# Output stores issued two products later in a fused attention and MLP kernel

## The chip, the cores and the metric

The kernel runs on one core of a Trainium2 chip. The time is device time in microseconds from one launch to its end; lower is better. The engines named below are TensorE (matrix products; PE in the profile, PEld for its weight loads), VectorE (DVE), ScalarE (ACT), GpSimd (POOL) and SyncE (SP). SyncE does no arithmetic here: it issues nearly all transfers between the memories, one after another, in the order in which the program wrote them. An engine runs its own list in order and meets the others only at semaphores.

## The reference

Eight batches of attention with 12 heads, 448 tokens and 64 elements a head, with q and k normalised by their root mean square, followed by a two-layer MLP on the joined heads:

```python
q_n, k_n = rmsnorm(q, g_q), rmsnorm(k, g_k)
attn = softmax(q_n @ k_n.T / sqrt(64)) @ v        # 8 x 12 x 448 x 64
x = attn.transpose(0, 2, 1, 3).reshape(3584, 768)
h = x @ w_in                                      # 768 -> 2048
g = h - tanh(h)
out = g @ w_out                                   # 2048 -> 768
```

All inputs and the output are float32 (in the kernel's launch, float64 weights are handed over as pairs of 32-bit words and rounded on the chip).

## The kernel before

The program writes all engines' lists out in one pass, without a scheduler. It goes over 48 attention steps, one for a batch and a pair of heads, and between the pieces of a step it lets a generator, `mlp`, put so many matrix products of an earlier batch into TensorE's list. So the MLP of batch b stands between the attention of batch b+1, and the MLP of the last batch stands alone at the end.

**The MLP.** For the first batch the projection is computed plainly (`project_first`): six chunks of 128 output columns, each of sixteen matrix products (L939), turned and stored one after another. During it the second half of the weights is still being rounded: SyncE loads raw words (L276), ScalarE, VectorE and GpSimd work on them in turn (L71, L78 to L82, L90), and the finished factors are copied out to memory (L359).

For the other batches both layers are computed by a scheme of seven products instead of eight: the rows of `ORDER`, 1, 5, 6, 2, 3, 7, 4, run through `products` (matmuls on L774). A hidden set is one run through the seven, with six matrix products in each; there are four sets in a batch. A projection has three runs with eight in each. A matrix product shows as two instructions in the profile. Each product needs a weight tile that is loaded from memory into one of six slots in a ring. At the start of product n the program writes the load of the tile of product n+4 into SyncE's list (`ring_load`, L397 for the first layer and L399 for the second). Since there are six slots, that load waits until TensorE has finished product n-2.

**The stores.** A projection run makes two chunks of 128 output columns. The first is complete after product 3, the second after product 4. What remains to be done for a chunk is put into `late["todo"]`, and runs after the matmuls of the following product have been written. It is `store`: VectorE turns the chunk in blocks of 32 by 32 (L869) into a tile `th`, of which there are two in rotation, and SyncE issues four transfers to the output (L872), of which the first waits for the turn. In SyncE's list they stand where the program is at that moment, so everything written later, whether a weight tile, v (L115, L125) or q and k (L462), is issued after them. The same two `th` tiles are used for tanh in the hidden layer (L810), and ScalarE waits there for a store that still reads its tile.

**What else hangs on SyncE.** q and k of a later step are loaded by eight transfers (L462), the first of which waits until VectorE has scaled the step whose buffer they take (L495). Each transfer also waits for the one eight places before it, since eight semaphores go round.

Of the kernel before, what the change touches and what calls it, by code (L numbers as in the profile page):

```python
# [144 lines left out]
def bounded_path(tc, ctx, q, k, v, moe_w_in, moe_w_out, out, g_col, ident, ones, half_ones, neg_half, early):  # L145
# [17 lines left out]
    nc = tc.nc  # L163
    B, H, S, D = q.shape
    DFF, DM = moe_w_out.shape
    P = 128
    CP = S // NCH
    NP = H // 2
    CD, CF = DM // P, DFF // P
# [11 lines left out]
    BL = 32  # L181
# [4 lines left out]
    def pool(name, **kw):  # L186
        return ctx.enter_context(tc.tile_pool(name=name, **kw))
# [17 lines left out]
    def bank_of(name):  # L205

        turns[name] += 1
        return banks[name][turns[name] % len(banks[name])]

    def mm_bank():  # L210
        return bank_of("mm")
# [29 lines left out]
    def built(j, p):  # L241

        if j == 2:
            return ring[:, p * 2 * HALF : (p + 1) * 2 * HALF].rearrange("p (f n) -> p f n", f=2)
        return w_half[j == 1][p]

    def w_out_row(f, i):
        return w_half[i][f // 2][:, f % 2]
# [54 lines left out]
    def weight(to):  # L303

        while done[1] < min(to, PIECES):
            n = done[1]
            round_weight_a(nc, raws[n], weight_dst(n))
            if n:
                round_weight_b(nc, raws[n - 1], weight_dst(n - 1))
            done[1] = n + 1  # L310
            finish_weights(n)
            load_weights(n + (3 if n < EARLY - 3 else 4))
            if kept[1] < kept[0] and n >= 4 * kept[0] + 2:
                keep_weights()
        if done[1] == PIECES > done[2]:
            round_weight_b(nc, raws[PIECES - 1], weight_dst(PIECES - 1))
            finish_weights(PIECES)
# [15 lines left out]
    def combine(count):  # L333
        for j, p, dst, x, y, op in combos[:count]:
            nc.vector.tensor_tensor(out=dst, in0=x, in1=y, op=op)
            if p == 7:
                kept[0] = j + 1
        del combos[:count]
# [7 lines left out]
    def combine_w_out(f):  # L346

        a11, a21 = (w_out_row(f, i) for i in range(2))
        a12, a22 = (w_out_row(f + HF, i) for i in range(2))
        t = [ring_slot() for _ in range(2)]  # L350
        s3, s1, s2, s4 = (t[i // 2][:, i % 2 * HALF : (i % 2 + 1) * HALF] for i in range(4))
        nc.vector.tensor_tensor(out=s1, in0=a21, in1=a22, op=ALU.add)
        nc.vector.tensor_tensor(out=s3, in0=a11, in1=a21, op=ALU.subtract)
        nc.vector.tensor_tensor(out=s2, in0=s1, in1=a11, op=ALU.subtract)
        nc.vector.tensor_tensor(out=s4, in0=a12, in1=s2, op=ALU.subtract)
        late["keep"].append(lambda: [keep_factors(3 + 2 * i, 2, f, t[i]) for i in range(2)])
# [7 lines left out]
    def keep_w_out(n):  # L364

        if not CF <= n < PIECES:
            return
        f, i, src = weight_piece(n)
        if f >= HF or i == 0:
            blk = i + 1 if f >= HF else 0  # L370
            for r in range(2):
                keep_factors(blk, 1, f % HF + r, src[:, r])
# [3 lines left out]
    def ring_slot():  # L376
        n = slots[0] % SLOTS
        slots[0] += 1
        return ring[:, n * SLOT : (n + 1) * SLOT]
# [10 lines left out]
    def ring_load(to):  # L390

        for n in range(len(ring_tiles), min(to, len(ring_steps))):
            b, layer, j, p = ring_steps[n]
            t = ring_tiles[ring_steps[n]] = ring_slot()
            if layer == 0:
                assert kept[1] > j
                nc.sync.dma_start(out=t[:, : 2 * HALF], in_=w_in_dram[j, p])  # L397
            else:
                nc.sync.dma_start(out=t, in_=w_out_dram[:, BLOCKS[p], j].rearrange("p f d -> p (f d)"))  # L399
# [339 lines left out]
    late = {}  # L739
# [7 lines left out]
    def part(name):  # L747
        return tp.tile([P, 2, HS], F32, name=name)
# [4 lines left out]
    def products(b, layer, count, width, depth, moving, done_with):  # L753

        took = 4 * HS / ENGINE_NS
        banks = {}  # L760

        def product(j, p, bank, first):
            if b == 0:
                weight(due[7 * j + ORDER.index(p)])
                combine(1)
                while any(c[:2] == (j, p) for c in combos):
                    combine(1)
                w = built(j, p).rearrange("p f (n d) -> p (f n) d", d=P)
            else:
                ring_load(ring_steps.index((b, layer, j, p)) + 5)  # L770
                w = ring_tiles[b, layer, j, p].rearrange("p (n d) -> p n d", d=P)
            for f in range(width):
                for c in range(depth):
                    nc.tensor.matmul(  # L774
                        bank[:, f * HS : (f + 1) * HS], lhsT=w[:, c * width + f, :], rhs=moving[p](c),
                        start=(first and f == 0 and c == 0), stop=(f == width - 1 and c == depth - 1),
                        skip_group_check=not first,
                    )
                    if f < width - 1 or c < depth - 1:
                        yield took  # L780
            now = late["todo"]
            late["todo"] = []
            for fn in now:
                fn()

        for j in range(count):
            use = done_with(j)
            for p in ORDER:
                first = p not in (2, 3, 7)
                bank = banks[p] = mm_bank() if first else banks[{2: 1, 3: 5, 7: 6}[p]]  # L790
                yield from product(j, p, bank, first)
                use(p, bank)
                yield took
# [69 lines left out]
    def store(b, n, y):  # L863

        o = part("th").rearrange("p f s -> p (f s)")
        nc.vector.transpose(out=o, in_=y if b >= FIRST else y.rearrange("r (c p) -> r p c", c=NCH))  # L869
        for i in range(P // BL):  # L870
            d = n * P + i * BL
            nc.sync.dma_start(  # L872
                out=out[b * S : (b + 1) * S, d : d + BL].rearrange("(j t) d -> t j d", t=BL),
                in_=o[i * BL : (i + 1) * BL].rearrange("t (j d) -> t j d", d=BL),
            )

    def project(b):
        g, t = late["g"], late["t"]
# [33 lines left out]
    def project_first(b):  # L912

        g = late["g"]
        for fn in late["todo"]:
            fn()
        late["todo"] = []
        took = 4 * S / ENGINE_NS
        for m in range(CD * CF):
            k, f = m // CF, m % CF  # L920
            n = (k + HC) % CD
            if f == 0:
                bank = mm_bank()
            if k < HC:
                weight(CF + HF + HF * (m + 1) // (HC * CF))
            elif m < HC * CF + 2:
                keep_w_out(PIECES - 2 + m - HC * CF)
            elif (m - HC * CF) % 4 == 0 and m - HC * CF <= 4 * HF:
                for fn in late["keep"]:
                    fn()  # L930
                late["keep"] = []
                combine_w_out((m - HC * CF) // 4 - 1)
            elif m == CD * CF - 12:
                ring_load(2)
                for fn in late["keep"]:
                    fn()
            elif m == CD * CF - 10:
                ring_load(4)
            nc.tensor.matmul(  # L939
                bank[:, :S], lhsT=w_out_row(f, n // HC)[:, n % HC * P : (n % HC + 1) * P], rhs=g[:, f, :],  # L940
                start=(f == 0), stop=(f == CF - 1),
            )
            if f == CF - 1:
                y = part("s2").rearrange("p f s -> p (f s)")
                nc.scalar.copy(out=y, in_=bank[:, :S])
                store(b, n, y)
            yield took
        wp_stack.close()
        late["tg"] = pool("tg", bufs=1)
        late["blocks"] = pool("blocks", bufs=1)  # L950

    def mlp():
        late["todo"], late["keep"] = [], []
        for b in range(B):
            yield from hidden(b)
            yield from project(b) if b else project_first(b)
        for fn in late["todo"]:
            fn()

    stream = mlp()  # L960
    spent = [0.0, 0.0]

# [383 lines left out]
def kernel(  # L1346
# [77 lines left out]
    with tc.If(bounded) as cmp:  # L1424
        with ExitStack() as arm, tc.manual_schedule():
            bounded_path(tc, arm, q, k, v, moe_w_in, moe_w_out, out, g_col, ident, ones, half_ones, neg_half, early)
# [34 lines left out]
```

## Time and profile before

| quantity | value |
|---|---|
| three runs | 1387.53, 1391.36, 1393.45 us |
| median | 1391.36 us |
| profiled execution | 1391.79 us |
| its span, first to last instruction | 1390.0 us |
| TensorE busy | 1352.7 us |
| VectorE busy | 892.2 us |
| mean granted TensorE clock | 0.992 |
| output stores, L872 | 192 transfers of 56 KB, median 1.9 us to landing |
| w_in tiles, L397 | 196 transfers of 384 KB, median 3.6 us to landing |
| w_out tiles, L399 | 147 transfers of 512 KB, median 4.4 us to landing |
| share of the transfer engines' time in use, one queue | 65.8% |

The span is 1.8 us shorter than the time of the same execution, which also has what lies around the instructions. In a row of the profile, "line engine operation out<-in" names a group of instructions; in a row of waits the numbers are the us in total, the times and the longest in us. A timeline row has the start, the duration, and in brackets the idle time before it with what ended it. The engine SPq is SyncE's queue: its busy time there is that of issuing a transfer, not of the transfer.

### The profile page before, as it was taken

How to read it: one execution, taken by the hardware profiler on the slowest of the kernel's cores; microseconds unless marked ns; L12 is line 12 of the kernel's file. 1: busy time of each engine (PE TensorE's matmuls, PEld its weight loads, DVE VectorE, ACT ScalarE, POOL GpSimd, SP SyncE). 2: the span in 40 equal slices, each digit the busy share in tenths (PEclk: the TensorE clock that was granted, in tenths of full speed). 3: DMA queues.
4: the chain of work that ended last, by engine and by line, in shares of the span. 5: the costliest groups of instructions: out<-in, count | busy, mean ns of one | idle time of the engine just before them, and what ended most of it. 6: DMA issues, size and time to landing. Idle time of an engine off the chain costs nothing. (4 is left out here: it accounts for less than half of the span.)

```text
span 1390.0 us, 29929 instructions
## 1 busy us (share of the span) xinstructions
PE 1352.7 (97%) x11840; PEld 1128.9 (81%) x11840; DVE 892.2 (64%) x1378; ACT 552.3 (40%) x1314; POOL 554.8 (40%) x345
## 2 busy tenths in 40 slices
PE   7989899999999999999999999999999999999997
PEld 3458654478998898898889889988988988899997
DVE  4999888856864677567766568546775677533311
ACT  7855554244433443334433444334433344311100
POOL 4746565225632356224552346323562245302300
PEclk9999999999999999999999999999999999999999
DMA  7879788775667566666657756675666666456663
GB/s 174 193 211 245 250 232 214 211 194 153 172 175 191 156 177 180 170 144 201 187 134 178 199 149 174 182 183 155 179 177 172 148 206 177 108 181 185 192 192 90
DMA packets 367656, 249.90 MB, mean 180 GB/s; under 512 B 281748, under 2 KB 309780, under 8 KB 367508
## 3 DMA queue, kind: packets, MB, share of 16 engines
q1 hardware_dynamic: 367504, 247.90, 65.8%
q8 instruction: 96, 1.57, 0.5%
q14 instruction: 52, 0.43, 0.1%
q10 hardware_dynamic: 4, 0.00, 0.0%
HBM read 214.40 MB, written 33.42 MB: 178 GB/s over the span
## 5 line engine op out<-in xcount | busy, mean ns | idle before, releaser
L774 PE MATMUL mm<-xT,w_f 128*128 128x224 f32 x1392 | 275.6, 354 | 0.0
L774 PEld LDWEIGHTS mm<-xT,w_f 128*128 128x128 f32 x1392 | 262.2, 190 | 10.2 <-issue 10.2
L774 PEld LDWEIGHTS mm<-gT,w_f 128*128 128x128 f32 x1344 | 252.8, 190 | 12.8 <-issue 8.4
L774 PE MATMUL mm<-gT,w_f 128*128 128x224 f32 x1344 | 263.0, 354 | 0.0
L811 POOL TENSOR_TENSOR gT<-s,th 128x448 f32<-128x448 f32 x96 | 120.1, 1260 | 332.1 <-ACT th L810 331.8
L531 PE MATMUL sc<-qT,kT 64*32 64x448 f32 (+1 forms) x3072 | 217.3, 503 | 10.3 <-ACT p_last L537 9.3
L488 POOL TENSOR_TENSOR rr_mine<-rr_mine,neg_half 128x28 f32<-128x28 f32 x33 | 158.2, 4794 | 147.9 <-DVE rr_mine L486 97.1
L774 PE MATMUL mm<-tt,w_f 128*128 128x224 f32 x1044 | 208.9, 353 | 3.8 <-DMA w_f<-w_in 3.8
L774 PEld LDWEIGHTS mm<-tt,w_f 128*128 128x128 f32 x1044 | 196.7, 190 | 9.8 <-issue 6.3
L774 PE MATMUL mm<-tg,w_f 128*128 128x224 f32 x1008 | 197.5, 352 | 0.0
L774 PEld LDWEIGHTS mm<-tg,w_f 128*128 128x128 f32 x1008 | 190.7, 190 | 0.0
L531 PEld LDWEIGHTS sc<-qT,kT 64*32 64x32 f32 x3072 | 71.1, 107 | 78.8 <-issue 56.5
L712 DVE TENSOR_TENSOR xT<-xT,sc 128x448 f32<-128x448 f32 x35 | 21.7, 621 | 138.9 <-PE sc L531 94.7
L597 PE MATMUL sc<-p,v_nat 64*32 64x448 f32 x1120 | 110.5, 536 | 0.0
L734 POOL TENSOR_TENSOR tt<-xT,tt 128x224 f32<-128x224 f32 x23 | 31.2, 1357 | 168.9 <-DVE xT L716 147.1
L537 ACT ACTIVATE p<-sc 128x448 f32<-128x448 f32 x132 | 71.9, 545 | 51.5 <-PE sc L531 39.0
L687 ACT COPY sum_g<-sum 32x14 f32<-32x14 f32 x280 | 56.3, 201 | 56.2 <-DVE sum L679 44.9
L939 PE MATMUL mm<-gT,w_out 128*128 128x448 f32 x192 | 76.0, 551 | 0.3 <-POOL w_out L90 0.3
L810 ACT ACTIVATE th<-s 128x448 f32<-128x448 f32 x96 | 54.5, 573 | 49.4 <-DVE s L840 26.6
L939 PEld LDWEIGHTS mm<-gT,w_out 128*128 128x128 f32 x192 | 36.3, 193 | 38.3 <-issue 35.8
L597 PEld LDWEIGHTS sc<-p,v_nat 64*32 64x32 f32 x1120 | 40.6, 107 | 31.0 <-issue 31.0
L537 ACT ACTIVATE p_last<-sc 128x224 f32<-128x224 f32 x66 | 20.0, 355 | 113.9 <-PE sc L531 113.9
(151 smaller groups left out, 1858.7 us busy)
## 6 DMA issues: line engine op xcount, KB each, us to landing
w_f<-w_in SPq DMA_DIRECT2D x196, 384.0 KB, 3.6
w_f<-w_out SPq DMA_DIRECT2D x147, 512.0 KB, 4.4
w_raw<-in_moe_w_out_dram SPq DMA_DIRECT2D x16, 768.0 KB, 5.1
out_dram<-th SPq DMA_DIRECT2D x192, 56.0 KB, 1.9
w_in<-w_out SPq DMA_DIRECT2D x21, 384.0 KB, 5.9
qk_nat<-in_q_dram SPq DMA_DIRECT2D x132, 56.0 KB, 3.1
qk_nat<-in_k_dram SPq DMA_DIRECT2D x132, 56.0 KB, 2.5
v_nat<-in_v_dram SPq DMA_DIRECT2D x72, 96.0 KB, 3.7
```

The costliest lines, as they stand in the source:

```text
L488: nc.gpsimd.tensor_tensor(out=mine, in0=mine, in1=neg_half[:, :1].to_broadcast([P, 2 * NJ]), op=ALU.pow)
L531: nc.tensor.matmul(tiles[h][i * BL : (i + 1) * BL, :n], lhsT=kT[r, c * P + at : c * P + at + BL], rhs=qT[r, first : first + n], start=True ...
L537: nc.scalar.activation(p[:, h, c if c < 2 else 0, :], tiles[h][:, :n], AF.Exp, scale=1.0 if rr is None else rr[:, 0, 2 * c + h : 2 * c + h ...
L597: nc.tensor.matmul(av[g][i * BL : (i + 1) * BL, :S], lhsT=v_nat[keys, h, c, m * BL : (m + 1) * BL], rhs=p[keys, h], start=first, stop=True ...
L687: nc.scalar.copy(out=acc[h * BL : (h + 1) * BL, g], in_=part[g * BL : (g + 1) * BL, h * NJ : (h + 1) * NJ])
L712: nc.vector.tensor_tensor(out=x, in0=x, in1=av[1][:, :S], op=ALU.add)
L734: eng.tensor_tensor(out=t2, in0=x22, in1=t1, op=ALU.subtract)
L774: nc.tensor.matmul(bank[:, f * HS : (f + 1) * HS], lhsT=w[:, c * width + f, :], rhs=moving[p](c), start=(first and f == 0 and c == 0), sto ...
L810: nc.scalar.activation(th, h, AF.Tanh, bias=0.0, scale=1.0)
L811: eng.tensor_tensor(out=g[:, rows, cols], in0=h, in1=th, op=ALU.subtract)
L939: nc.tensor.matmul(bank[:, :S], lhsT=w_out_row(f, n // HC)[:, n % HC * P : (n % HC + 1) * P], rhs=g[:, f, :], start=(f == 0), stop=(f == C ...
```

## The change

The turn on VectorE stays where it is. The four transfers of a store are no longer written at once: they go into a list, `late["out"]`, with a count of two. At the start of each product of batches 2 to 8, just after the ring load of that product, every count goes down by one, and a store whose count is at zero is written. So a store stands behind the ring loads of the next two products. In the projection of the first batch the list is emptied in the middle of the next chunk, ahead of its ninth matrix product. What is left at the end of the MLP is written there.

```diff
             else:
                 ring_load(ring_steps.index((b, layer, j, p)) + 5)
+                step_out()
                 w = ring_tiles[b, layer, j, p].rearrange("p (n d) -> p n d", d=P)
...
         o = part("th").rearrange("p f s -> p (f s)")
         nc.vector.transpose(out=o, in_=y if b >= FIRST else y.rearrange("r (c p) -> r p c", c=NCH))
-        for i in range(P // BL):
-            d = n * P + i * BL
-            nc.sync.dma_start(
-                out=out[b * S : (b + 1) * S, d : d + BL].rearrange("(j t) d -> t j d", t=BL),
-                in_=o[i * BL : (i + 1) * BL].rearrange("t (j d) -> t j d", d=BL),
-            )
+
+        def issue():
+            for i in range(P // BL):
+                d = n * P + i * BL
+                nc.sync.dma_start(
+                    out=out[b * S : (b + 1) * S, d : d + BL].rearrange("(j t) d -> t j d", t=BL),
+                    in_=o[i * BL : (i + 1) * BL].rearrange("t (j d) -> t j d", d=BL),
+                )
+
+        late["out"].append([2, issue])
+
+    def step_out(by=1):
+        for entry in late["out"]:
+            entry[0] -= by
+        while late["out"] and late["out"][0][0] <= 0:
+            late["out"].pop(0)[1]()
...
             if f == 0:
                 bank = mm_bank()
+            if f == CF // 2:
+                step_out(2)
...
     def mlp():
-        late["todo"], late["keep"] = [], []
+        late["todo"], late["keep"], late["out"] = [], [], []
         for b in range(B):
             yield from hidden(b)
             yield from project(b) if b else project_first(b)
         for fn in late["todo"]:
             fn()
+        step_out(2)
```

On every engine but SyncE the order of the instructions is the same as before.

## The prediction

> **What bounds the kernel now.** I read the busy shares first.
>
> ```profile
> PE 1352.7 (97%) x11840; PEld 1128.9 (81%) x11840; DVE 892.2 (64%) x1378; ACT 552.3 (40%) x1314; POOL 554.8 (40%) x345
> ```
>
> TensorE sets the time, so the change is worth what it takes from, or adds to, TensorE's idle time and slow time after 203 us, where the first store is issued (the changed instructions start there). Next the windows, from 290 us (the second batch) to the last matmul, and the five us after the pause discussed below (columns: length, busy time of PE, PEld, DVE, ACT, POOL, granted clock, DMA share, GB/s):
>
> ```profile
> 290.00:1382.00 1092.00, 1087.92 (x9151) 969.31 (x9142) 655.35 (x1036) 388.64 (x1008) 402.88 (x245) 1.00 0.63 172
> ...
> 237.30:242.10 4.80, 4.80 (x20) 2.07 (x21) 4.59 (x8) 1.45 (x3) 4.01 (x4) 0.64 0.83 193
> ```
>
> In 1092 us TensorE idles 4.1 us: little is left there. TensorE's own waits (us in total, times, longest), and SyncE's queue's:
>
> ```profile
> PE sc L531 <- ACT p_last L537: 9.3, 3, 5.4
> ...
> PE mm L774 <- DMA w_f<-w_in: 3.8, 5, 2.0
> ```
>
> ```profile
> SPq L872 <- DVE th L869: 252.6, 45, 12.2
> ...
> SPq L462 <- DVE qk_n L495: 63.7, 16, 8.6
> ```
>
> SyncE stands 252.6 us before stores whose turn is not done, but TensorE loses only 3.8 us to late w_in tiles. The gain is bounded by TensorE's column, not SyncE's. By window, the five waits are 0.3, 2.0, 0.3, 0.8 and 0.3 us, one in each of five 180 us batches from 300 us on. All lie at the same place, the seventh product of a batch's first w_in set. The timeline of the last of them:
>
> ```profile
> 1103.72 1.09 DVE L495 TENSOR_TENSOR qk_n<-qk_nat,rr_mine 128x896 f32<-128x896 f32 x1
> 1104.73 0.64 DVE L869 STREAM_TRANSPOSE th<-s 128x448 f32<-128x448 f32 x1
> ...
> 1097.09 0.54 SPq L397 DMA_DIRECT2D w_f<-w_in  x1
> 1105.40 1.95 SPq L872 DMA_DIRECT2D out_dram<-th  x4
> 1107.45 0.44 SPq L397 DMA_DIRECT2D w_f<-w_in  x1
> 1107.98 1.95 SPq L462 DMA_DIRECT2D qk_nat<-in_q_dram  x4
> 1109.97 2.19 SPq L462 DMA_DIRECT2D qk_nat<-in_k_dram  x4
> 1112.27 6.42 SPq L397 DMA_DIRECT2D w_f<-w_in  x7
> ...
> 1115.83 2.51 PE L774 MATMUL mm<-tt,w_f 128*128 128x224 f32 x12 [0.32 <-DMA w_f<-w_in]
> ```
>
> SyncE issues a w_in tile at 1097.5, then stands to 1105.4 before the batch's last store (its turn is queued on VectorE behind the attention's work), then issues store, tile, eight q/k loads and at 1112.3 the tile that TensorE waits for at 1115.5.
>
> The other wait after 203 us is in the first batch:
>
> ```profile
> 223.97 2.04 POOL L90 TENSOR_TENSOR w_out<-w_out,w_raw 128x768 int32<-128x768 int32 x1 [2.27 <-ACT w_out L71]
> ...
> 221.72 0.37 SPq L276 DMA_DIRECT2D w_raw<-in_moe_w_out_dram  x1
> 222.19 2.14 SPq L872 DMA_DIRECT2D out_dram<-th  x4
> 224.43 1.84 SPq L115 DMA_DIRECT2D v_nat<-in_v_dram  x2
> 226.32 2.06 SPq L125 DMA_DIRECT2D v_nat<-in_v_dram  x2
> ...
> 229.64 0.46 SPq L276 DMA_DIRECT2D w_raw<-in_moe_w_out_dram  x1
> ...
> 234.81 0.89 ACT L71 ACTIVATE w_out<-w_raw 128x768 f32<-128x768 f32 x1 [6.47 <-DMA w_raw<-in_moe_w_out_dram]
> ...
> 237.30 1.23 PE L531 MATMUL sc<-qT,kT 64*32 64x448 f32 x14 [2.14 <-ACT p_last L537]
> ```
>
> A store and four v loads stand ahead of a raw weight load. ScalarE waits 6.47 us for that load, with the exponentials that free the score banks queued behind it, and TensorE waits 2.14 us. In the window from that point on, the granted clock is 0.64.
>
> **What the Trainium skill says.** "DMA: Bandwidth & Descriptors", section "Anatomy of one DMA", says that a semaphore wait happens on the issuing sequencer before dispatch. That is what the 8 us hole between 1097.6 and 1105.4 shows. "TensorE: Matmul & The Clock Gate", Part 1, says the clock is halved after an idle window of about 3.4 us, and full again after as long a busy one. The trace agrees on the size (0.64 over 4.8 us is 1.7 us lost, half of 3.4 us), but here 2.1 us of recorded idle was enough; I use the trace.
>
> **The change, part by part.** The store's four DMAs, their waits and their sizes stay; so do all orders on the other engines. Only SyncE's order changes.
>
> *Batch ends (batches 2 to 6, where attention still runs beside the next batch).* New order: three w_in tiles, the fourth, v, the fifth, the store of product 3's chunk, the sixth, q/k, the seventh, the last store. The earlier of the two stores is now ready when reached (its turn ended at 1091.64). The sixth tile needs only product 4 of the old batch (finished near 1096.3, as VectorE's L905 reads it then), the seventh product 1 of the new one (1105.7). The q/k loads still wait for VectorE's L495, which ends at 1104.8: SyncE's stand doesn't go, it goes over to them. Eight issues take 1.95 + 2.19 plus gaps, 4.2 us, so the seventh tile goes out near 1109.1 instead of 1112.3: 3.2 us earlier, where at most 2.0 us of idle is to be covered. In the worst batch one q issue is 1.7 us slow (3.68 against 1.95); the same 3.2 us remain, and 1.0 is spare. The five waits go: 3.8 us of idle, plus for each the overlap of matmul records, 354 ns long at a spacing of 189 (148.52 us for 784 in the chain): 5 x 0.16 = 0.8. **Sum 4.6 us.**
>
> What is late next: the last store's four issues (2.0 us) now stand ahead of the next set's first tile. It goes out near 1111.6 instead of 1112.8, so nothing moves later. The cover for its 3.6 us landing is product 4, which ends about 1118.2.
>
> *Between batch ends.* Stores in the middle of a projection also go behind two tiles. Where q/k loads come between, a following tile goes out up to 2.0 us (four issues) later than it would without the store; tiles go out about five products ahead (8 x 2 x 0.189 = 3.0 us each, 15 us), land after 4.4 us, and no wait stands there now. Cost 0. Without cover it would be 2 us each.
>
> *First batch.* The second store moves from ahead of the v loads to behind the q/k loads. The raw load then has four DMAs of v and two of w_out ahead: six issues at 0.5 to 0.6 us from 222.1, so 225.5; its buffer is free when POOL's L90 ends at 226.01. So 226.0 instead of 229.64: 3.6 us earlier. With the same 5.2 us to landing ScalarE gets it at 231.2, runs L71, L72, L945 and the exponentials (1.99 us from 234.81 to 236.80, then 0.79), limited by the score matmuls ending near 231.5, and is done near 234.0; TensorE needs it at 234.7. The pause goes, with 0.7 us to spare: 2.14 us plus the overlap of records there (536 ns long at 54 spacing), 0.5, so 2.6, plus 1.7 of half clock. **Sum 4.3 us.** The first store moves behind two raw loads that wait on POOL anyway (holes from 207.9 to 209.9 and 211.4 to 215.2), and lands well before its buffer is turned into again at 237.8. Later ones move among weight copies that no matmul near them reads: 0.
>
> *The end.* The last tiles are issued by 1365.1, so the late stores meet an empty queue; the last turn (1382.64) still precedes four issues of 2.12 us. 0.
>
> *Unknown: the stores' new company.* Each store writes 229 KB in 128-byte pieces right among weight loads; before, it often went out alone. From no effect (DMA share 0.63) to one tile late by the difference of longest and median landing of w_f, 8.1 - 4.1 = 4.0 us at each of five ends; a spare of 1.0 to 2.9 leaves 1 to 3 us in one or two ends, 0 to 4 us in all. I take 0.
>
> Total 8.9 us. Against the profiled execution's own 1391.79 this is 1382.9. That execution lies 0.4 us above the median of the runs shown, 1391.36; the forecast is **1383.0 us**. A measurement can tell about 0.5% (7 us) of this kernel from no change; 1384.4 is the line.
>
> **Rivals.**
>
> *Half the gain.* The first-batch pause depends on a landing under full DMA load (0.83) with 0.7 us to spare; a landing of 6 us brings it back, and any pause can halve the clock. Then only the 4.6 us go: 1387. For it: the fastest run, 1387.53, is 4.3 us under the profiled one, as if the pause weren't in every execution. Against: 3.6 us of lead. The same figure follows if the pause goes and the batch ends keep their waits.
>
> *The transfers are hidden anyway.* SyncE's wait goes to the q/k loads and the ring still comes late: 1390 to 1392. For it: the 8.6 us waits on L495 stay. Against: the 3.2 us worked out above, all of them issue time and a turn that no longer come first.
>
> *The change doesn't delay what it says.* If the countdown released stores in the same slot, nothing would move: 1391. Against: on SyncE's queue one or two tile loads, and the q/k group, change places with them.
>
> *A new wait, slower than before.* The last store's buffer (th, two of them) is next written by ScalarE's tanh, at 1114.05 now. The store is issued by about 1111.6 and lands after 1.9 us, at 1113.5: 0.5 us to spare. If it lands late, tanh waits, and the exponentials of the next visit (1124.29) behind it. ScalarE idles 1.62, 0.82, 0.16 and 3.11 us between, 5.7 us of cover. It decides from a landing of 1.9 + 0.5 + 5.7 = 8.1 us on; the longest store took 5.2. Five ends each 4 us beyond that would be 20 us, less 8.9: 1403.
>
> **How the numbers follow.** Both gains: 0.50, at 1381 to 1385.5 (its own range). One of the two: 0.27, at 1386 to 1389. Hidden, or no move: 0.14, at 1389.5 to 1392.5. Slower: 0.09, to 1403. The range for 8 in 10 goes from 1380.5 (one half-clock spell fewer by chance, 1.7 us) to 1392, which takes in the unknown 4 us as well. Faster by over 0.5% needs nearly all of the first case: 0.47. Within 0.5%: 0.46. Slower by over 0.5%: 0.07.
>
> **What would show it.** Right: no TensorE wait for w_in after 290 us, and idle there under 0.5 us; the seventh tile of a batch end issued 3 us earlier against its product; the raw load issued near 226.0; no pause and no half clock near 237; SyncE's waits at the store well under 100 us, those at L462 as they are or more. Wrong: a wait of ScalarE's tanh for a store, a pause near 237 that stays, or a new TensorE wait for w_out tiles in the middle of a projection.

## The result, and the profile after

The changed kernel takes 1381.34 us, median of six runs from 1381.09 to 1382.10. The kernel before took 1392.28 us in the same comparison (1387.53 to 1393.45). The ratio is 0.9927, with a 95% interval from 0.9914 to 0.9941: 0.73% faster, 10.9 us between the medians. The forecast was 1383.0 us in a range from 1380.5 to 1392.0. The profiled execution took 1382.10 us with a span of 1380.2 us, against 1391.79 and 1390.0 before.

Lines have moved in the changed kernel: the matmul of the products is L775 (before L774), the turn L870 (L869), the stores L875 (L872), tanh L811 (L810), the copy behind a first-batch projection L958 (L945) and its matmul L952 (L939).

The busy shares of the kernel after:

```profile
PE 1347.5 (98%) x11840; PEld 1127.5 (82%) x11840; DVE 891.1 (65%) x1378; ACT 551.7 (40%) x1314; POOL 553.7 (40%) x345
```

TensorE is still the bound, and its busy time fell by 5.2 us with the same 11840 instructions. Of this, 1.0 us lies in the first 190 us, where nothing is changed. Behind that, matmul records that overlap a stall, and the half clock, at which matmuls are longer, are gone (3.0 us by the prediction's estimates of 0.8, 0.5 and 1.7); the rest was not taken apart.

TensorE's waits in the kernel after, from 203 us to the end of the work (us in total, times, longest), are a single one:

```profile
PE sc L531 <- ACT p L537: 0.3, 1, 0.3
```

Before, there were also the five for w_in tiles and the pause of 2.14 us in the same stretch.

By stretches (length, busy time of PE, PEld, DVE, ACT, POOL, granted clock, DMA share, GB/s), TensorE of the kernel after idles 0.04 us from the second batch to the end, where it idled 4.1 before, and 232 to 237 us, where the pause was, is full and at full clock:

```profile
290.00:1372.00 1082.00, 1081.96 (x9109) 966.35 (x9107) 650.75 (x1037) 384.41 (x1002) 401.76 (x245) 1.00 0.64 172
232.00:237.00 5.00, 5.00 (x63) 2.38 (x53) 4.76 (x8) 3.17 (x7) 2.86 (x3) 1.00 0.94 230
```

The waits of SyncE's queue in the kernel after (those before stores for other things than the turn, some 10 us in all, are left out):

```profile
SPq L397 <- PE mm L775: 238.0, 126, 6.8
...
SPq L462 <- DVE qk_n L495: 184.7, 31, 8.9
...
SPq L875 <- DVE th L870: 16.8, 3, 10.6
```

SyncE's stand before stores fell from 252.6 us to 16.8, and at the same time its stand before q and k loads rose from 63.7 to 184.7. Half of the stand went there, most of the rest to the weight tiles (L397 from 206.2 us to 238.0, L399 from 119.3 to 190.2). SyncE still stands; what changed is who is behind it.

The timeline of the batch end that the prediction showed, in the kernel after (VectorE, SyncE, TensorE):

```profile
1094.07 1.09 DVE L495 TENSOR_TENSOR qk_n<-qk_nat,rr_mine 128x896 f32<-128x896 f32 x1
1095.08 0.64 DVE L870 STREAM_TRANSPOSE th<-s 128x448 f32<-128x448 f32 x1
...
1095.22 1.89 SPq L462 DMA_DIRECT2D qk_nat<-in_q_dram  x4
1097.16 2.04 SPq L462 DMA_DIRECT2D qk_nat<-in_k_dram  x4
1099.30 0.42 SPq L397 DMA_DIRECT2D w_f<-w_in  x1
1099.82 2.05 SPq L875 DMA_DIRECT2D out_dram<-th  x4
...
1105.68 2.43 PE L775 MATMUL mm<-tt,w_f 128*128 128x224 f32 x12
```

SyncE starts at the end of L495, not at the end of the turn. The seventh tile is issued at 1099.30, 6.4 us ahead of its product at 1105.68. Before, it was issued at 1112.27 for a product that could have started at 1115.3 (1115.83 less the stall of 0.5), a lead of 3.1 us. The prediction had 3.2 us of gain here; it is 3.3.

The first batch in the kernel after (SyncE, ScalarE, TensorE):

```profile
225.50 0.37 SPq L276 DMA_DIRECT2D w_raw<-in_moe_w_out_dram  x1
...
230.12 2.39 SPq L875 DMA_DIRECT2D out_dram<-th  x4
...
231.11 0.94 ACT L71 ACTIVATE w_out<-w_raw 128x768 f32<-128x768 f32 x1 [3.32 <-DMA w_raw<-in_moe_w_out_dram]
...
233.22 0.79 ACT L537 ACTIVATE p_last<-sc,rr 128x224 f32<-128x224 f32 x2
...
233.69 1.02 PE L531 MATMUL sc<-qT,kT 64*32 64x448 f32 x16
```

The raw load goes out 4.1 us sooner on the clock of the profile, ScalarE has it 3.7 us sooner, and the score matmuls, which were cut into two and fourteen by 2.14 us of idle time, run as one group of sixteen.

**Where the time went, by position.** Both kernels run the same 11840 matmuls in the same order, so the start of each can be subtracted from the start of the same one in the other trace. Against the kernel after, the kernel before is late by 0.5 us at 220 us (nothing is changed ahead of that but the first store; the runs below lie between 1.0 us ahead of the kernel after and 0.7 us behind it there), by 5.2 at 240, still 5.2 at 455, 5.8 at 615, 8.0 at 780, 9.7 at 945 and 10.2 at 1370. The gain of the first batch is thus 4.7 us, that of the later batches 5.0. The tail takes 0.4 us more in the kernel after, which leaves the 9.8 us between the spans. The experiments below are read in the same way, as "first" and "later" loss against the kernel after.

### The profile page after: what moved, and what is told of

Read it like the earlier page. It is cut to its first block, busy times and chain, and to the rows that moved or that the text cites. A ratio compares the mean times of both kernels' runs of the same rounds, so it can differ in the third digit from the quotient of the medians.

```text
span 1380.2 us, 29907 instructions
## 1 busy us (share of the span) xinstructions
PE 1347.5 (98%) x11840; PEld 1127.5 (82%) x11840; DVE 891.1 (65%) x1378; ACT 551.7 (40%) x1314; POOL 553.7 (40%) x345
## 4 chain that ended last, share of the span: by engine, by line
PE 89%; DVE 5%; DMA 2%; SPq 2%; ACT 1%; issue 1%; POOL 0%; ACTq 0%; DVEq 0%
PE mm L775 67%; PE sc L531 8%; PE sc L597 6%; PE mm L952 5%; PE sc L585 1%; PE sc L635 1%; DVE w_out L335 1%; DVE rs L663 1%; DMA gT<-in_moe_w_in_dram 1%; DMA w_raw<-in_moe_w_in_dram 1%; DVE w_out L82 1%; SPq L125 1%; DMA w_in<-w_out 1%; DVE xT L719 0%; PE mm L635 0%
## 5 line engine op out<-in xcount | busy, mean ns | idle before, releaser
L775 PE MATMUL mm<-xT,w_f 128*128 128x224 f32 x1392 | 275.6, 354 | 0.0
L775 PEld LDWEIGHTS mm<-xT,w_f 128*128 128x128 f32 x1392 | 262.1, 190 | 10.2 <-issue 10.2
L775 PEld LDWEIGHTS mm<-gT,w_f 128*128 128x128 f32 x1344 | 252.8, 190 | 12.8 <-issue 8.4
L775 PE MATMUL mm<-gT,w_f 128*128 128x224 f32 x1344 | 263.0, 354 | 0.0
L775 PE MATMUL mm<-tt,w_f 128*128 128x224 f32 x1044 | 208.6, 353 | 0.0
L775 PEld LDWEIGHTS mm<-tt,w_f 128*128 128x128 f32 x1044 | 197.0, 190 | 4.4 <-issue 4.4
L775 PE MATMUL mm<-tg,w_f 128*128 128x224 f32 x1008 | 197.5, 352 | 0.0
L775 PEld LDWEIGHTS mm<-tg,w_f 128*128 128x128 f32 x1008 | 190.7, 190 | 0.0
L811 ACT ACTIVATE th<-s 128x448 f32<-128x448 f32 x96 | 54.5, 573 | 69.6 <-DVE s L841 30.2
L952 PE MATMUL mm<-gT,w_out 128*128 128x448 f32 x192 | 74.6, 543 | 0.3 <-POOL w_out L90 0.3
L952 PEld LDWEIGHTS mm<-gT,w_out 128*128 128x128 f32 x192 | 35.7, 190 | 37.3 <-issue 34.9
L142 POOL TENSOR_TENSOR rr<-rr,neg_half 112x8 f32<-112x8 f32 (+1 forms) x30 | 49.0, 1660 | 34.2 <-DVE rr L141 34.1
```

The source lines that it names most:

```text
L142: nc.gpsimd.tensor_tensor(out=r, in0=r, in1=neg_half[:rows], op=ALU.pow)
L775: nc.tensor.matmul(bank[:, f * HS : (f + 1) * HS], lhsT=w[:, c * width + f, :], rhs=moving[p](c), start=(first and f == 0 and c == 0), sto ...
L811: nc.scalar.activation(th, h, AF.Tanh, bias=0.0, scale=1.0)
L952: nc.tensor.matmul(bank[:, :S], lhsT=w_out_row(f, n // HC)[:, n % HC * P : (n % HC + 1) * P], rhs=g[:, f, :], start=(f == 0), stop=(f == C ...
```

## The experiments

The theory: two wait chains go, each because one store no longer stands ahead of a load, and the rest of the 48 stores does nothing. The rivals: only one of the two parts is real; the middle stores matter; it is the bytes of the stores, not their place; and, for a longer delay, a new wait of tanh. In the diffs the lines are those of the changed kernel, except where the kernel before is named.

### One part alone: the first batch, the later batches

```diff
-        late["out"].append([2, issue])
+        if b == 0:
+            late["out"].append([2, issue])
+        else:
+            issue()
```

> Only the first batch's stores are late; those of the other batches are issued as before. If the two gains are separate and sized as the two traces say (4.7 us by 285 us of the span, 5.0 us after it), this is 4.7 us faster than before, 1387.5 against 1392.3: no pause and no half clock near 237 us, and the five waits for w_in tiles at the batch ends still there, 3.8 us in all. If the later gain depends on the first (a program shifted against its transfers), it is the whole 10 us or much less than 4.7.

Measured: 1388.73 us against 1392.33, ratio 0.9975 [0.9966, 0.9983]. By position: first 0.0 us lost, later 4.6. The clock near 237 is full, and the w_in waits are there:

```profile
PE mm L775 <- DMA w_f<-w_in: 1.5, 3, 0.6
```

At the second batch end, where the longest stood before, TensorE waits 1.8 us, which the profile puts down to VectorE.

The other half has `if b > 0` in the same place.

> Only the stores of batches 2 to 8 are late. Separate gains: 5.0 us faster than before, 1387.3; the pause of 2.1 us near 237 us and the half clock of 3.4 us after it stay, and no TensorE wait for w_in is left. If the pause in the first batch comes and goes from run to run by itself, some runs are near 1383.

Measured: 1386.46 us, ratio 0.9955 [0.9942, 0.9969]. By position: first 4.6 us lost, later 0.0. There is no w_in wait, and the pause of the first batch is as it was (ScalarE and TensorE of this kernel):

```profile
233.76 0.89 ACT L71 ACTIVATE w_out<-w_raw 128x768 f32<-128x768 f32 x1 [6.37 <-DMA w_raw<-in_moe_w_out_dram]
...
236.25 1.34 PE L531 MATMUL sc<-qT,kT 64*32 64x448 f32 x14 [2.04 <-ACT p_last L537]
```

The two parts are both real, do not depend on each other, and add up to the whole. The rival "half the gain" is out. One thing stays open: the fastest of this run's five executions took 1383.04 us at a mean clock of 0.995, the other four 1384.85 to 1387.34 at 0.992 to 0.993. So there are executions with less half clock, there or in the first 200 us; no trace of one was taken.

### Which stores

Late only with `if b > 0 and n == CD - 1`, the last chunk of a batch, one store in six:

> Late is only the last store of each of the batches 2 to 8, one of six. If only SyncE's order at the batch ends counts, this has the whole later gain, 5.0 us, 1387.3. If each late store helps a little (less standing on SyncE, 252 us before), it has about a sixth to a third of it, 1390.5 to 1391.5.

Measured: 1384.42 us, ratio 0.9947 [0.9933, 0.9960], 2.9 us less than expected; the interval overlaps that of the run with all later stores late, and three of the five executions have a mean clock of 0.995 or 0.996. By position first 4.3 us lost, later 0.0. TensorE has no w_in wait, though SyncE's stand at the stores is nearly what it was before:

```profile
SPq L875 <- DVE th L870: 208.8, 39, 12.2
```

The counterpart, `if b > 0 and n < CD - 1`:

> The other five stores of each of the batches 2 to 8 are late, the last one is issued as before. If only the last store counts: no gain, 1392.3 within 1 us, and the waits for w_in at the batch ends stay near 3.8 us in all, although SyncE's standing before stores falls by more than half. If standing anywhere costs time: 3 to 4 us faster, 1388.5.

Measured: 1393.71 us, ratio 1.0011 [1.0002, 1.0020]; by position first 5.4 us lost (the pause is 2.9 us long in this trace), later 4.9. So there is no gain; the median is even 1.4 us above that of the kernel before, a little more than the 1 us expected. SyncE's stand at stores falls to 83.8 us, and TensorE has its waits all the same:

```profile
PE mm L775 <- DMA w_f<-w_in: 3.0, 4, 1.6
```

So moving five sixths of the stores of the later batches gains nothing, and the part of SyncE's stand that matters is worth 5 us of 252.6.

In the first batch, one store late, the second, `if b == 0 and n == HC + 1`:

> Late is one store of the 48: the second of the first batch, which goes from ahead of four v loads to behind the q and k loads. If the pause near 237 us comes from the raw load standing behind this store on SyncE, this has the whole first gain, 4.7 us: 1387.5 against 1392.3, the raw load issued near 226.0, no half clock there. If the first store's bytes or several stores together make the landing late, less than 2 us of it.

Measured: 1387.86 us against 1391.59, ratio 0.9978 [0.9970, 0.9985]; by position first 0.1 us lost, later 5.1. The raw load goes out at 225.14, the pause and the half clock are gone: the whole of the first part, from one store.

Both together, six stores of 48, `if (b == 0 and n == HC + 1) or (0 < b < 6 and n == CD - 1)`:

> Six of the 48 stores late and no others: the second one of the first batch, and the last one of each of the batches 2 to 6. Theory (each part of the gain comes from one store a place, and the other 42 late stores do nothing): no TensorE wait for w_in tiles after 290 us, no pause near 237, 1381 to 1382.5 us, ratio about 0.993. Rival (the gain of the parts that were tried alone does not add up, or the middle stores help when the others are late too): 1384 us or more. SyncE's waits before stores should stay long, 200 us or more, in either case.

Measured: 1380.89 us against 1390.50, ratio 0.9929 [0.9915, 0.9943]; by position the same as the kernel after at every point from 190 us on (0.5 us ahead throughout, from the stretch before). SyncE stands 211.5 us before stores:

```profile
SPq L875 <- DVE th L870: 211.5, 40, 12.2
SPq L462 <- DVE qk_n L495: 98.6, 21, 8.6
```

The other 42 stores contribute nothing. This kernel and the changed one are equal within what the intervals tell.

### The place or the bytes

The kernel before, with every store in its old place, but the six stores found above send only the first of their fourteen row blocks, so that most of six chunks of the output isn't written:

```diff
+        few = 1 if (b == 0 and n == HC + 1) or (0 < b < 6 and n == CD - 1) else NJ
...
-                in_=o[i * BL : (i + 1) * BL].rearrange("t (j d) -> t j d", d=BL),
+                in_=o[i * BL : (i + 1) * BL].rearrange("t (j d) -> t j d", d=BL)[:, :few],
```

with the same `[:, :few]` on the output's side.

> Order as before. Six stores, the second of the first batch and the last of batches 2 to 6, send one fourteenth of their rows (the other rows of those chunks are left out of the output): same four issues in the same place, same wait for the turn, 16 KB instead of 229 KB each. If the place on SyncE counts (issue time and the wait for the turn), the waits stay: 1390 to 1392.5. If it is the stores' bytes that delay the landings beside them, the gains come as with the change: 1382 to 1385, and in the first batch the raw load lands 2 us sooner after an unchanged issue.

Measured: 1387.05 us, ratio 0.9971 [0.9964, 0.9978], between the two answers. By position 1.9 us are lost in the first batch (of 4.7) and 3.9 in the later ones (of 5.0). The waits of TensorE:

```profile
PE sc L531 <- ACT p_last L537: 7.1, 3, 4.9
...
PE mm L774 <- DMA w_f<-w_in: 2.7, 5, 1.1
```

All five w_in waits are there, 2.7 us instead of 3.8. In the first batch the raw load still takes 5.3 us from its issue to ScalarE's start on it (232.27 less 226.99), as with the full stores (5.2): there is no sign that the stores' bytes slow it. But it is issued 1.3 us sooner against TensorE than in the kernel before: the store's four issues take 1.80 us instead of 2.14, and the first two v loads behind it, each of which waits for the transfer eight places before, 0.94 instead of 1.84. That the transfers they wait for are done sooner is inferred, not measured alone. The recorded pause shrinks to 1.0 us, and with it the half clock is gone. So the place is most of it in the later batches; in the first batch the size of the store counts too, through SyncE's issue time, and a little of it goes far, because the half clock hangs on it.

### The rival of a new wait: a longer delay

The prediction's rival on the slower side was a late store whose tile tanh needs. To bring it about, the count was doubled:

```diff
-        late["out"].append([2, issue])
+        late["out"].append([4, issue])
```

and both `step_out(2)` became `step_out(4)`.

> The count is four products instead of two in batches 2 to 8 (first batch as in the change). If two are enough and later costs nothing: 1381.3, equal to the change within 0.5 us. If the rival of the prediction has any weight (a tanh of ScalarE waiting for a late store that still reads its th tile), ScalarE waits at L811 for stores in this trace, up to some 5 us at a batch end; by the cover of 5.7 us TensorE still loses nothing. A loss of over 1 us would show the cover smaller than worked out.

Measured: 1398.88 us, ratio 1.0061 [1.0048, 1.0074], slower than the kernel before. By position 0.7 us is lost in the first batch and 17.9 later, 2.9 to 4.7 at each of the five batch ends. ScalarE's waits in this kernel:

```profile
ACT th L811 <- DMA out_dram<-th: 21.7, 4, 6.6
...
ACT th L811 <- POOL gT L812: 19.6, 6, 3.8
```

and its timeline at the second of the ends:

```profile
621.64 2.08 SPq L875 DMA_DIRECT2D out_dram<-th  x4
...
624.86 2.11 SPq L875 DMA_DIRECT2D out_dram<-th  x4
...
626.18 0.54 ACT L811 ACTIVATE th<-mm 128x448 f32<-128x448 f32 x1 [5.58 <-DMA out_dram<-th]
...
638.71 0.58 ACT L811 ACTIVATE th<-s 128x448 f32<-128x448 f32 x1 [3.81 <-POOL gT L812]
...
639.60 0.61 ACT L537 ACTIVATE p_last<-sc 128x224 f32<-128x224 f32 x2
```

The first tanh of the new batch waits for a store. It can't be the one issued from 624.86 on, whose last issue ends after tanh has begun; it is the one from 621.64, the last chunk but one. The wait is 5.6 us where tanh waited 1.8 us for its product in the kernel after:

```profile
618.64 0.54 ACT L811 ACTIVATE th<-mm 128x448 f32<-128x448 f32 x1 [1.75 <-PE mm L775]
```

Everything in the chain moves by the 3.8 us between: the second tanh, the work of VectorE and GpSimd on the result, then the fourth tanh, which waits for GpSimd, and behind it on ScalarE the exponentials, for which TensorE stops. The end costs 3.8 us by position. At the other four, too, the loss is the delay of the first tanh to within 0.1 us.

Which of the two stores does it? Doubled for the last store alone, `[4 if 0 < b < 6 and n == CD - 1 else 2, issue]`:

> As the change, but the last store of each of the batches 2 to 6 is issued four products later instead of two, some 2 us later than in the change; the others stay at two. It frees the th tile of the second tanh of the batch after. If the loss of the run with four everywhere (17.9 us after 285 us of the span, against the change) came from this tile, it is here again, 10 us or more. If it came from the tile of the first tanh, and the 5.7 us of cover of the prediction's rival hold for the second one: within 1 us of the change, 1381 to 1382.5, with a wait of ScalarE's second tanh of up to 2 us in the trace.

Measured: 1382.27 us, ratio 0.9932 [0.9916, 0.9949]; by position no loss. Tanh waits for no store. So it isn't the last store, the one of the prediction's rival.

Doubled for the other store of the last run alone, `n == HC - 1`:

> As the change, but the last store but one of each of the batches 2 to 6 is issued four products later, which brings it from ahead of the q and k loads to behind them, 8 us later or more. It frees the th tile of the first tanh, which now also stands behind VectorE's read of a bank that product 4 needs. If this is where the run with four everywhere lost its time: most of the 17.9 us again, 1394 to 1400, with waits of ScalarE at L811 for stores of 4 to 6 us at each of five batch ends. If it is not: 1381 to 1384.

Measured: 1387.24 us, ratio 0.9965 [0.9954, 0.9976]; by position 6.3 us lost in the later batches, not most of the 17.9 as expected but a third. ScalarE's waits:

```profile
ACT th L811 <- DMA out_dram<-th: 26.6, 5, 6.6
...
ACT th L811 <- POOL gT L812: 0.6, 1, 0.6
```

The store's wait is as long as with all stores four late, where the profile puts the fifth of these waits, 5.2 us, down to TensorE. But the fourth tanh no longer waits for GpSimd. ScalarE in the kernel before, at the exponentials of the last end, and then in this kernel at the second end:

```profile
1124.29 0.61 ACT L537 ACTIVATE p_last<-sc 128x224 f32<-128x224 f32 x2 [3.11 <-PE sc L531]
```

```profile
624.48 0.54 ACT L811 ACTIVATE th<-mm 128x448 f32<-128x448 f32 x1 [5.68 <-DMA out_dram<-th]
...
634.89 0.60 ACT L537 ACTIVATE p_last<-sc 128x224 f32<-128x224 f32 x2 [0.81 <-PE sc L531]
```

Of a wait for TensorE of 3.11 us, 0.81 us is left, and the first tanh's delay of 3.9 us costs 1.6. At the five ends, delays of 2.9 to 4.8 us cost 0.4 to 2.8. With the wait for GpSimd ahead of the exponentials, none of that cover is left. It takes both waits in one chain to make the large loss.

The wait for GpSimd is there in the kernel after too, where it costs nothing (before: 0.6 us, once):

```profile
ACT th L811 <- POOL gT L812: 19.7, 6, 3.8
```

It goes with the order in which the tiles `th` are handed out, which can be read from the addresses in the built programs. In the kernel after, and with the last stores at four products or with them alone late, tanh 1 to 5 of the new batch use the same tile one after another; with all stores at four it is tanh 1 to 4. So the fourth can't begin before GpSimd has read the third's result. With the last store but one alone at four only the first three share a tile, with the last store at one product only the first two, and in the kernel before the two tiles alternate. Why the tiles are handed out in this way was not found out. A third tile was not tried.

Last, half the delay for the last store, `[1 if 0 < b < 6 and n == CD - 1 else 2, issue]`:

> As the change, but the last store of each of the batches 2 to 6 is issued one product later instead of two: behind the sixth w_in tile, still ahead of the q and k loads. SyncE's wait for its turn costs little, since the q and k loads wait for nearly the same moment (L495 ends 0.6 us before the turn); its four issues of 2.0 us still delay the seventh tile. So of the 5.0 us of the later gain nearly all goes again: the five waits for w_in come back with 3 to 4 us in all, 1385 to 1387. If being late at all is enough: 1381.3.

Measured: 1385.49 us, ratio 0.9956 [0.9939, 0.9972]; by position 2.8 us lost in the later batches, not nearly all of the 5.0 as expected, though the median lies in the range expected. Two waits of TensorE show:

```profile
PE mm L775 <- DVE s L837: 1.3, 1, 1.3
PE mm L775 <- DMA w_f<-w_in: 0.6, 1, 0.6
```

The store stands ahead of the q and k loads again, but the sixth tile, which stood behind it before, is already out. So the delay works in steps. By position, one product gives 2.2 us, two give 5.0, four for the last store no more than two, and four for all stores lose more than was gained.

## Why the prediction was right

**Batch ends, 4.6 us.** Right in mechanism and in place: the five waits are gone, the seventh tile goes out 3.3 us earlier against its product (3.2 predicted), and SyncE's stand went over to L462 as it said, though only half of it. The size was 5.0 us in the traces: the overlap of records at each wait, put at 0.16 us, is 0.24 on average (5.0 less the 3.8 of idle time, over five). It is 4.6 to 5.1 us in the runs that keep these waits. On the medians it is larger: the runs with only the first batch's store or stores late lie 6.5 and 7.4 us above the kernel after (the kernel before took 1391.59 and 1392.33 us beside them, 1392.28 beside the kernel after). Their executions scatter, from 1384.4 to 1390.1 with all stores of the first batch late (two at the same mean clock of 0.995 differ by 4.5 us), while the six of the kernel after lie within 1.0 us. So the stalls seem not to be of fixed size, and the prediction sized them from one execution, in which they may have been small. That would account for part of the gain of 10.9 us between the medians where the sum was 8.9 (8.4 against the median shown). Another part is plain: the profiled execution of the kernel after is the slowest of its six, 0.8 us above their median, and that of the kernel before lies 0.5 us below its own. That the stalls vary is inferred from the scatter; no trace of a long execution was taken, and why they would vary stays open.

**First batch, 4.3 us.** Right in mechanism and place; it measured 4.7 by position. The raw load was said to go out at 226.0; it did at 225.50, in an execution 0.53 us ahead there. But the pause costs more than its recorded 2.14 us and the 0.5 of overlap. In the kernel before two score matmuls ran alone ahead of it:

```profile
234.22 0.94 PE L531 MATMUL sc<-qT,kT 64*32 64x448 f32 x2
```

When the exponentials are done in time, the second of the sixteen starts 0.01 us after the first (in the runs with the first batch's stores late, with the last store at four and with six stores). So the other fourteen could have started at 234.23, not at the 234.7 of the prediction, and did at 237.30. That is 3.1 us; with 1.7 of half clock it makes 4.8, where 4.7 was measured. The estimate of 1.7 us stands by the run with the small stores, too, which has no half clock: it lost 1.9 us by position, and this wait, read in the same way, is 1.95.

The spare of 0.7 us did not hold, and that no pause came was partly luck. The landing took 5.6 us, not 5.2. In the run that keeps the pause TensorE resumes 0.50 us after the start of the exponentials (236.25 less 235.75). In the kernel after they start at 233.22, so the score matmuls were free at 233.72, hardly later than they could have begun (the first is at 233.69). Other runs with this order show what a longer landing does: 5.3 to 5.5 us cost nothing; 5.9, 6.2 and 6.4 us (the last store at one product, all at four, the last but one at four) cost 0.3, 0.7 and 0.8 us by position. So the landing of 6 us in the rival "half the gain" does bring a wait back, but a small one, and none of these had the half clock behind it.

**Middle stores, 0; the end, 0.** Right: with all but the last stores of the later batches late nothing was gained, and with six of 48 late nothing was missing. The tail cost 0.4 us, within what one execution differs from another.

**The unknown, the stores' company, taken as 0.** Right. The late stores land later (a median of 3.6 us instead of 1.9, at most 5.9), but the tiles among them don't: 4.0 us in the median and 7.7 at most, 4.1 and 8.1 before.

**The rival of a new wait was priced wrongly**, though it didn't decide. Three of its terms failed. It named the last store and the tanh at 1114.05 as a pair, with 0.5 us to spare; with the last store four products late nothing waited, because the tile is next taken by the sixth tanh of the batch. The pair that can meet is the store before it and the first tanh. It counted 5.7 us of ScalarE's idle time as cover. Only the last piece of that, 3.11 us of waiting for TensorE, can be: with the last store but one alone at four, 2.0 to 2.5 us of each delay were covered. The first two pieces, 1.62 and 0.82 us, cover nothing: they are waits for VectorE's sums, which stand on VectorE behind the work on tanh's result, and at the second end they are as long with the delay as in the kernel after, 1.50 and 0.57 us. And it said all orders on the other engines stay. They do, but the tiles behind the orders don't: the new wait for GpSimd, 19.7 us of ScalarE's time, was in no step of the prediction. It uses up the 3.11 us, so that with all stores at four each end lost as much as its tanh was late. The mechanism itself was right, and at twice the delay it makes the kernel slower than before.

## What to carry to other kernels

Don't value a queue's stand by its length. Ask for each stop what is queued directly behind it and whether that is late for its user: here 5 us of 252.6 mattered, at five stores, a sixth, before which SyncE hardly stood, cost 4.7 us by its place, and the other 42 could stay. When a delay is to be covered by another engine's idle time, see first what that idle time waits for; where it is waiting for what comes after the delayed work, it moves along and covers nothing, and a second wait can use up the rest. And a delay of a release isn't done with the orders of the engines: look at which buffer each later step then gets.

## What was not expected of the hardware

- The half clock came after 2.0 to 2.9 us of recorded idle time of TensorE (before, and the runs that keep the pause), where "TensorE: Matmul & The Clock Gate" of the Trainium skill, Part 1, has an idle window of about 3.4 us. A pause of 1.0 us in the same place didn't bring it. The length of a pause isn't all: in the clock records of each of the thirteen traces the spells of half clock begin whole multiples of 3.413 us from one another (before: 19.46, 94.55, 166.23 and 237.91 us), and, but for the last at the end of the work, they take one such window of 3.41 us or several. Of the windows at full clock, all with 2.0 us or more of recorded idle time were followed by half clock, none with less than 1.5 us was, and between the two both occurred. What decides there is not known.
- One SyncE issue of the same tile load took from 0.32 to 2.30 us in the kernel after (median 0.35). The long ones were not taken apart.
